# A scheduled attention kernel whose list of steps is given other step times, another order for the steps that empty PSUM, and more zero products

## The chip, the cores and the metric

The kernel runs on one core of one Trainium2 chip. The metric is the device time of one execution in microseconds, as the median of several runs. The engines are TensorE (PE; PEld is its weight load), VectorE (DVE), ScalarE (ACT), GpSimd (POOL) and SyncE (SP, which issues most DMAs).

## The reference

Two attention blocks over the same input are mixed by a gate. Both have 2048 positions, a model width of 512 and 32 heads of 16.

```python
def reference(A_x, A_wqkv, A_wo, B_x, B_wqkv, B_wo, gate_w):
    x = A_x                                              # 1 x 2048 x 512, bf16
    g = _sigmoid((x * gate_w).sum(-1, keepdims=True))
    a = _A_ref(x, A_wqkv, A_wo)    # full attention: softmax(q k^T / 4) v, then @ wo
    b = _B_ref(x, B_wqkv, B_wo)    # each position sees itself and 7 others: back 2, 4, ... 14
    return g * a + (1 - g) * b
```

The full attention has 32 heads x 2048 x 2048 exponentials; they are the bulk of the work.

## The kernel before

**Block A.** Heads are taken in eight groups of four, queries in four chunks of 512. One group with one chunk is a period; the last one is halved. In a period there are 16 key tiles x 4 heads = 64 units. A unit is the scores of 128 keys by 512 queries (one product of TensorE with 32 rows, `qk`), their exponential, and the product with V (`pv`), which adds into an accumulator, one PSUM bank for a period. Four heads stand in four strips of TensorE's rows or columns, so that up to four such products run beside each other.

Most units go to ScalarE in sets of alternately three and two (`set_sizes`): the scores go to a ring in PSUM (`rA` of three banks, `rB` of two), ScalarE writes the exponentials to `pT`. A ring is free again when its exponential is done. Some units go elsewhere instead. VectorE computes the exponential in four passes that read the scores' bank (`p1` to `p4`, tiles `dg` and `pd`): each needs the one before. GpSimd does the same with a cubic after a copy by VectorE (`g1`, then `g2` to `g4`, tiles `gt`). A unit taken so is a block; its scores are a `dq` product.

**PSUM.** Five banks are the two rings. The other three (`bank`, tag `m`) serve everything else: the accumulator, the blocks' scores, and the results of all projections, which VectorE copies out.

**Block B.** For each of 16 tiles of 128 positions K, V and Q are projected and copied (`kvs`, `qb`); K and V go to DRAM and come back shifted (`sh`); GpSimd does products and sums, with a small softmax between (`mx`, `lg`, `rr`). The gate's products go through DRAM as well (`zd`, `zfin`) and meet the outputs at their normalisation.

**The list.** The order on each engine is not the program's own: every step is an `Op` with an engine, an assumed time `occ`, a due time `dl`, the steps that it needs (`deps`), and the buffers that it takes and uses. `Scheduler.run` plays the program through with these times. At each turn it looks which engine can start a step first, and takes, among the steps of that engine that can start within `AHEAD`, the one with the lowest `key` (its due time, shifted by the drift of the whole list). `Feeder` adds the sets and the blocks while the list is being made: a new block is asked for when few passes of the last are left, so a VectorE that the list thinks faster gets more blocks, and ScalarE fewer sets. `t1` spreads the periods' due times. The result is an order for each engine. The chip keeps that order and its own times: TensorE, for example, stands at a product whose bank isn't free, with all that is listed behind it. `pick_pe` tries to keep the scores ahead of other products when the exponential would come late; a product whose strips are free costs only `JOIN` there, 0.05, and another kind of product `SWITCH` more.

A pass that needs another step on its own engine could start, in the list before, at that step's end:

```python
o.ready = max([o.rel] + [d.end if d.eng == o.eng and o.eng in ("dve", "act", "pool") else d.done for d in o.deps]
              + [d.t for d in o.after])
```

**Zero products.** After the list is made, `add_zeros` looks at each stretch of `SPAN` = 3.42 us. Where TensorE's work takes less than the share `STREAM` of it, it puts products of zeros (`z`), which add nothing to an open accumulator, into gaps of TensorE's list.

**Steps that come up later.** `sel` (tile `selp`, from `kmp`) runs four times, once for each two groups of heads, as a maximum of four numbers and a scaled mask on VectorE. `k_pack` and `q_pack` project the K and Q of two groups at a time into `kpk` and `qpk`.

Nearly every instruction is recorded at one line, that of the helper which keeps the order (L379 in the profile of before), so groups are told apart by tiles.

Of the kernel before, what the change touches and what calls it, by code (L numbers as in the profile page):

```python
# [21 lines left out]
    t1=848.0,  # L22
# [13 lines left out]
NG = 8  # L36
# [69 lines left out]
SPAN, STREAM, SPARE, ROOM, FREE = 3.42, 0.49, 0.32, 0.1, 0.3  # L106
WARM = 13
WAVE, SWITCH, JOIN = 0.222, 0.10, 0.05
# [10 lines left out]
SET_LAT = 0.52  # L119
EARLY = 4  # L120
ACC = 100
SLOW = 1.5


class Scheduler:
# [56 lines left out]
    def key(self, o):  # L182
        return o.dl - (ACC if o.role == "acc" else 0.0) if o.role else o.dl + self.drift
# [145 lines left out]
def kernel(  # L329
# [85 lines left out]
    UNIT = 0.459  # L415
# [100 lines left out]
    o_init_d = op("dve", 2.2, init_dve, -9.0, deps=[o_init_z])  # L516
# [71 lines left out]
    o_kr, o_qr = {}, {}  # L588
# [6 lines left out]
    for sc in range(NC):  # L595
# [28 lines left out]
        km0_ops.append(op("dve", 0.7, km, -5.0 + sc, deps=[a, o_init_d], use=[tk]))  # L624
# [19 lines left out]
    def q_direct(c_, dl):  # L644
# [32 lines left out]
        a = op("dve", 1.1, qc, dl + 0.9, deps=[a] + o_cr[:1], use=[tk_q] + ([] if fold else [qt_tok[0]]),  # L677
# [7 lines left out]
        o_qr[0, c_] = [op("dve", 0.7, qe, dl + 3.0, deps=[a], alloc=[qt_tok[0]] if fold else [],  # L685
# [20 lines left out]
        st_f["rx"], st_f["th"] = op("dve", 1.4, rx, dl + 5.0, deps=[a, o_fpv], alloc=[t_h], use=[t_f, acc_tok["f"]]), t_h  # L706
# [7 lines left out]
    def k_pack(cc):  # L714
# [3 lines left out]
        for sc in range(NC):  # L718
# [23 lines left out]
            evs.append(op("dve", 0.7, kc, dl + 1.5, deps=[a], alloc=[] if sc else [tp], use=[tk] + ([tp] if sc else []),  # L742
                          after=pk_last[:]))
            pk_last[:] = evs[-1:]
            kms.append(op("dve", 0.7, km, dl + 3.0, deps=[evs[-1]], use=[tp]))
# [5 lines left out]
        kv_p[cc] = op("dve", 0.35, sel, dl + 4, deps=kms + [o_init_p3], slack=SLOW)  # L751
# [14 lines left out]
    def q_pack(cc):  # L766
# [5 lines left out]
        for c in range(NC):  # L772
# [18 lines left out]
            evs.append(op("dve", 0.7, qc, dl + 1.5, deps=[a], alloc=[] if c else [tp], use=[tk] + ([tp] if c else []),  # L791
# [19 lines left out]
        b = op("dve", 0.7, be, dl + 3.5, deps=[prev], alloc=[tbn], use=[tb])  # L811
# [33 lines left out]
    def v_proj(h0, h1, tb, TB, dl, rel, w, dep, use=(), P=2):  # L845
# [21 lines left out]
        c = op("dve", 0.75, ev, dl + 1.7, deps=[a, o_init_p if h1 <= 8 else o_init_p3], use=[tk])  # L867
# [31 lines left out]
    a = op("dve", 0.7, ze, 37.0, deps=[a], alloc=[tzo], use=[tkz])  # L899
# [34 lines left out]
    def b_tile(t):  # L934
# [29 lines left out]
        ka = op("dve", 0.71, ke, tb - 13, deps=[a], use=[tk, tkv])  # L964
# [3 lines left out]
        va = op("dve", 0.71, ve, tb - 11, deps=[a, ka], use=[tk, tkv])  # L968
# [9 lines left out]
        qa = op("dve", 0.71, qe, tb - 5, deps=[a], use=[tk, tqb])  # L978
# [83 lines left out]
        a = op("dve", 0.45, sm_pre, tb + 21, deps=[l1], alloc=[tmx], use=[tlg])  # L1062
        a = op("pool", 0.65, sm_sub, tb + 22, deps=[a], use=[tlg, tmx], lat=1.5)
        a = op("act", 0.3, sm_exp, tb + 24, deps=[a], use=[tlg])
        a = op("dve", 0.78, sm_post, tb + 25, deps=[a], alloc=[trr], use=[tlg])
# [15 lines left out]
        o_obt.append(op("dve", 0.44, oe, tb + 65, deps=[a], use=[tk]))  # L1081
# [80 lines left out]
    class Feeder:  # L1162
# [45 lines left out]
        def new_set(self, s):  # L1208
# [45 lines left out]
            b = Op("act", 0.427 * n + 0.081, ex, now + 1.0, deps=[a], alloc=[tp], use=[tr_], name=f"ex{k}", role="ex")  # L1254
# [98 lines left out]
        def d_passes(self, s, e):  # L1353
# [50 lines left out]
            if e == "d":  # L1404
                ps_ = [Op("dve", 0.69, p1, x + 1.0, deps=[o], alloc=[tg], use=[tk], role="d", name="p1")]
                ps_.append(Op("dve", 0.69, p2, x + 1.1, deps=ps_[-1:], use=[tk, tg], role="d", name="p2"))
                ps_.append(Op("dve", 0.69, p3, x + 1.2, deps=ps_[-1:], use=[tk, tg], role="d", name="p3"))
                ps_.append(Op("dve", 0.69, p4, x + 1.3, deps=ps_[-1:], alloc=[tp], use=[tk, tg], role="d", name="p4", slack=0.4))
            else:
                ps_ = [Op("dve", 0.69, g1, x - 2.0, deps=[o], alloc=[tg, tp], use=[tk], role="d", name="g1")]  # L1410
# [19 lines left out]
    for pi, (c_, i, q0, qn) in enumerate(periods):  # L1430
# [39 lines left out]
        a = op("dve", 0.75 * f if pi else 1.45, po1, E - 1.0, deps=[o_end[pi]] + ([] if pi else [st_f["rx"]]), alloc=[ta],  # L1470
               use=[acc_tok[pi]] + ([] if pi else [st_f["th"]]))
        a = op("dve", 0.4 if last else 0.25, po2, E + 2.0, deps=[a, o_g], alloc=[trd], use=[ta])
        a = op("dve" if last else "pool", 0.27 if last else 0.95, po2b, E + 3.0 if last else E + 2.5, deps=[a],
               alloc=[to] if par == 0 else [], use=[ta, trd] + ([to] if par else []))
        if par:
            o_oat[pr, c_, q0] = op("dve", 0.75 * f, po3, E + 4.0 if i == NG - 1 else E + 12.0, deps=[a], use=[to])

    st_fa = {}
    for t in range(NT):
# [40 lines left out]
        if fa:  # L1520
# [15 lines left out]
            fa0 = op("dve", 0.71, to_fa, dl, deps=[a] + ([fa0] if tt else []), alloc=[] if tt else [tfa], use=[tk] + ([tfa] if tt else []))  # L1536
# [3 lines left out]
            a = op("dve", 0.71, t_ev, dl, deps=[a, fa0], alloc=[tos], use=[tk2, tfa])  # L1540
# [5 lines left out]
        a = op("act" if on_act else "dve", 0.65 if on_act else 0.71, f_ev, dl + (1.0 if late else 0.0), deps=[a], alloc=[tos], use=[tk])  # L1546
# [40 lines left out]
```

## Time and profile before

| | us |
|---|---|
| median of three runs | 863.15 |
| the three runs | 866.37, 862.37, 863.15 |
| the profiled execution | 867.63 |
| its span, first to last instruction | 865.9 |
| mean granted TensorE clock | 0.988 |

In the rows of the profile, a group shows its tiles as written<-read, the shapes, the count, the busy time and the mean duration in ns, and the idle time before it with what ended it. A row of a timeline has the start, the length and what ran, with a count where several are merged. A row of a window has the stretch, its length, the busy time of each engine with the number of its instructions, the granted clock, the share of DMA and GB/s. A row of waits has who waited for whom: the sum in us, how often, the longest.

### The profile page before, as it was taken

The numbers are of one execution on the slowest core, as the hardware profiler recorded it, in microseconds if no ns is written. First come the engines' busy times: TensorE is split into PE (matmuls) and PEld (weight loads), VectorE is DVE, ScalarE is ACT, GpSimd is POOL, SyncE is SP. The second block draws the span as 40 slices with busy tenths as digits, with TensorE's granted clock in tenths as the row PEclk, the third lists the DMA queues.
The fourth block names the chain that finished last, engine by engine and source line by source line (L and its number), as shares of the span: only waits on it lengthen the run. The fifth ranks groups of instructions, "written<-read, shape, count | busy, mean of one in ns | idle before, by whom it ended". The sixth has DMA issues, their size and how long they took to land.

```text
span 865.9 us, 18130 instructions
## 1 busy us (share of the span) xinstructions
PE 794.5 (92%) x7145; PEld 258.5 (30%) x7145; DVE 749.8 (87%) x1235; ACT 841.4 (97%) x750; POOL 714.0 (82%) x588
## 2 busy tenths in 40 slices
PE   8999999998889998999999998989889889999997
PEld 3323333322223332222223332222222223222233
DVE  6788889889999998798999889898999986888875
ACT  5999999999999999899999999999999999999996
POOL 2086998899799989996998999899989768888772
PEclk9999999999999998899999999999999999999999
DMA  9432203231321113123113111323110000000000
GB/s 224 134 90 89 81 7 77 95 79 39 106 72 64 49 62 74 38 49 111 50 37 111 50 62 19 117 68 93 50 50 25 1 2 13 13 14 14 8 14 32
DMA packets 54781, 51.56 MB, mean 60 GB/s; under 512 B 13628, under 2 KB 51172, under 8 KB 54696
## 3 DMA queue, kind: packets, MB, share of 16 engines
q1 hardware_dynamic: 53496, 50.11, 20.1%
q8 instruction: 56, 0.92, 0.4%
q10 hardware_dynamic: 1200, 0.30, 0.2%
q14 instruction: 29, 0.24, 0.1%
HBM read 38.04 MB, written 6.33 MB: 51 GB/s over the span
## 4 chain that ended last, share of the span: by engine, by line
ACT 58%; issue 19%; PE 17%; DVE 3%; DMA 1%; SPq 1%; ACTq 0%; DVEq 0%
ACT pT L379 58%; PE bank L379 12%; PE ring L379 5%; DVE dg L379 1%; ACT lg L379 1%; DMA xT<-in_A_x_dram 1%; SPq L379 1%; DVE pd L379 0%; DVE kmp L379 0%; DVE kpk L379 0%; DVE rden L379 0%; DVE kvs L379 0%; DVE selp L379 0%; DVE qpk L379 0%; DVE oat L379 0%
## 5 line engine op out<-in xcount | busy, mean ns | idle before, releaser
L379 ACT ACTIVATE pT<-ring 128x1536 bf16<-128x1536 f32 x728 | 835.2, 1279 | 10.5 <-PE ring L379 8.7
L379 PE MATMUL ring<-qt,kt 32*128 32x512 bf16 (+1 forms) x1880 | 291.7, 379 | 42.0 <-ACT pT L379 36.3
L379 PE MATMUL bank<-pT,vp_all 128*17 128x512 bf16 (+2 forms) x1872 | 288.9, 379 | 19.0 <-ACT pT L379 15.5
L379 DVE SCALAR_TENSOR_TENSOR dg<-bank,dg 128x512 bf16<-128x512 uint16 x420 | 289.3, 689 | 12.9
L379 POOL TENSOR_TENSOR prod<-prod 128x1024 f32<-128x1024 f32 x144 | 230.9, 1603 | 11.3
L379 DVE TENSOR_SCALAR dg<-bank 128x512 bf16<-128x512 uint16 x210 | 142.8, 680 | 46.3 <-PE bank L379 33.3
L379 PEld LDWEIGHTS <-kt 32*128 32x128 bf16 x2136 | 96.1, 91 | 278.3 <-issue 272.0
L379 POOL TENSOR_TENSOR prod<-sh,qb 128x1024 f32<-128x1024 bf16 x64 | 135.1, 2132 | 39.0 <-DMA sh<-kv_scr 37.7
L379 PEld LDWEIGHTS <-vp_all 128*17 128x17 bf16 (+1 forms) x2112 | 93.3, 89 | 223.3 <-issue 197.4
L379 DVE TENSOR_TENSOR pd<-bank,dg 128x512 uint16<-128x512 f32 x210 | 144.5, 688 | 6.7
L379 POOL TENSOR_TENSOR prod<-sh,lg 128x1024 f32<-128x1024 bf16 x64 | 127.5, 2014 | 1.8
L379 PE MATMUL bank<-ones_t,z 128*32 128x512 bf16 (+1 forms) x367 | 119.4, 388 | 1.5 <-DVE ones_t L379 1.5
L379 PE MATMUL bank<-qt,kt 32*128 32x512 bf16 (+1 forms) x240 | 87.6, 377 | 2.0 <-DVE kvs L379 0.9
L379 POOL TENSOR_TENSOR gt<-gt 128x512 f32<-128x512 f32 x63 | 75.2, 1194 | 5.2
L379 PE MATMUL bank<-pd,vp_all 128*17 128x512 bf16 (+1 forms) x216 | 75.6, 379 | 0.0
L379 PE MATMUL bank<-bw,xT 128*32 128x512 bf16 x768 | 69.2, 388 | 0.1
L379 POOL TENSOR_SCALAR gt<-gt 128x512 f32<-128x512 uint16 (+2 forms) x63 | 38.9, 617 | 25.8 <-DVE gt L379 18.3
L379 PE MATMUL bank<-xT,wst 128*32 128x512 bf16 x512 | 46.0, 390 | 0.0
L379 PEld LDWEIGHTS <-z 128*32 128x32 bf16 x367 | 29.7, 96 | 37.3 <-issue 30.3
L379 PEld LDWEIGHTS <-xT 128*32 128x32 bf16 (+1 forms) x1088 | 31.6, 96 | 27.0 <-issue 22.3
L379 DVE STREAM_TRANSPOSE accT<-bank 128x512 f32<-128x512 f32 (+1 forms) x32 | 21.9, 686 | 10.3 <-PE bank L379 9.9
L379 DVE CAST kvs<-bank 128x512 bf16<-128x512 f32 x32 | 21.8, 683 | 3.2 <-PE bank L379 2.8
(103 smaller groups left out, 413.4 us busy)
## 6 DMA issues: line engine op xcount, KB each, us to landing
sh<-kv_scr SPq DMA_DIRECT2D x64, 512.0 KB
kv_scr<-kvs SPq DMA_DIRECT2D x16, 256.0 KB
out_dram<-osb SPq DMA_DIRECT2D x15, 128.0 KB
kt<-kpk SPq DMA_DIRECT2D x28, 64.0 KB
qt<-qpk SPq DMA_DIRECT2D x28, 64.0 KB
wst<-in_A_wqkv_dram SPq DMA_DIRECT2D x3, 512.0 KB
bw<-in_B_wqkv_dram SPq DMA_DIRECT2D x1, 1536.0 KB
bwo<-in_B_wo_dram SPq DMA_DIRECT2D x1, 512.0 KB
```

The source lines that it names most:

```text
L379: return chain_on(key, f(*a, **k))
```

## The change

All edits are in the list's numbers and in how it weighs steps; no engine's instructions are written differently. The step times of VectorE and ScalarE are set anew: passes from 0.69 to 0.61, copies from 0.7 to 0.61, an exponential from 0.427 n + 0.081 to 0.426 n + 0.052, `sel` from 0.35 to 1.2. On VectorE a step that needs another one of VectorE can start `RAW` = 0.115 after that one's end. The times from an engine's end to another's start (`LAT`, `SET_LAT`) change a little. A VectorE step without a role (all but the blocks' passes) that uses one of the three banks gets a key lower by `EV` = 100, so that it goes ahead of all else that can start. The blocks' scores are due earlier (`DQ_DL`, `GQ_DL`). `t1` falls from 848 to 828, and `STREAM` rises from 0.49 to 0.54.

```diff
-    t1=848.0,
+    t1=828,
...
+        self.frees = eng == "dve" and not role and any(not tk.res.fifo for tk in use)
...
-LAT = dict(pe=0.25, dve=0.12, act=0.22, pool=2.5, sp=2.2)
-AHEAD = dict(pe=0.10, dve=0.12, act=0.25, pool=0.5, sp=0.0)
+LAT = dict(pe=0.22, dve=0.135, act=0.165, pool=2.5, sp=2.2)
+RAW = 0.115
+AHEAD = dict(pe=0.10, dve=0.1, act=0.25, pool=0.5, sp=0.0)
...
-DQ_DL = 0.4
+DQ_DL = -1
+GQ_DL = -2
...
-SPAN, STREAM, SPARE, ROOM, FREE = 3.42, 0.49, 0.32, 0.1, 0.3
+SPAN, STREAM, SPARE, ROOM, FREE = 3.42, 0.54, 0.32, 0.1, 0.3
...
-SET_LAT = 0.52
+SET_LAT = 0.495
+EV = 100
...
-        o.ready = max([o.rel] + [d.end if d.eng == o.eng and o.eng in ("dve", "act", "pool") else d.done for d in o.deps]
+        o.ready = max([o.rel] + [d.end + (RAW if o.eng == "dve" else 0.0) if d.eng == o.eng and o.eng in ("dve", "act", "pool") else d.done for d in o.deps]
...
-        return o.dl - (ACC if o.role == "acc" else 0.0) if o.role else o.dl + self.drift
+        return o.dl - (ACC if o.role == "acc" else 0.0) if o.role else o.dl + self.drift - (EV if o.frees else 0.0)
...
-            lat = LAT[e] + occ if o.lat is None else o.lat
+            lat = LAT[e] + occ if o.lat is None else o.lat + (max(0.0, occ - o.occ) if e == "pe" else 0.0)
...
-    UNIT = 0.459
+    UNIT = 0.447
...
-        kv_p[cc] = op("dve", 0.35, sel, dl + 4, deps=kms + [o_init_p3], slack=SLOW)
+        kv_p[cc] = op("dve", 1.2, sel, dl + 4, deps=kms + [o_init_p3], slack=SLOW)
...
-            b = Op("act", 0.427 * n + 0.081, ex, now + 1.0, deps=[a], alloc=[tp], use=[tr_], name=f"ex{k}", role="ex")
+            b = Op("act", 0.426 * n + 0.052, ex, now + 1.0, deps=[a], alloc=[tp], use=[tr_], name=f"ex{k}", role="ex")
...
-            o = Op("pe", WAVE, None, max(s.free["pe"], s.free["dve"] - 1.0) + (DQ_DL if e == "d" else 1.5), alloc=[tk],
-                   lat=0.5, kind="r", name=e + "q", role="dq")
+            o = Op("pe", WAVE, None, max(s.free["pe"], s.free["dve"] - 1.0) + (DQ_DL if e == "d" else GQ_DL), alloc=[tk],
+                   lat=0.45, kind="r", name=e + "q", role="dq")
...
-                ps_ = [Op("dve", 0.69, p1, x + 1.0, deps=[o], alloc=[tg], use=[tk], role="d", name="p1")]
+                ps_ = [Op("dve", 0.61, p1, x + 1.0, deps=[o], alloc=[tg], use=[tk], role="d", name="p1")]
...
-                ps_ = [Op("dve", 0.69, g1, x - 2.0, deps=[o], alloc=[tg, tp], use=[tk], role="d", name="g1")]
+                ps_ = [Op("dve", 0.61, g1, x - 2.0, deps=[o], alloc=[tg, tp], use=[tk], role="d", name="g1")]
```

The other edits set further steps of VectorE to their new times in the same way (copies 0.61, `mx` 0.33, `rr` 0.72, `obt` 0.33, the accumulator's transposes 0.64 and 0.63, its reciprocal 0.17).

More of the change, by code (lines that the diff above doesn't have):

```diff
@@ L676, in q_direct @@
             a = op("pe", 0.265 * n, qp(c, n), dl, after=[a], use=[tk_q, tw0])
-        a = op("dve", 1.1, qc, dl + 0.9, deps=[a] + o_cr[:1], use=[tk_q] + ([] if fold else [qt_tok[0]]),
+        a = op("dve", 0.95, qc, dl + 0.9, deps=[a] + o_cr[:1], use=[tk_q] + ([] if fold else [qt_tok[0]]),
                alloc=[ta_q] + tqf)
@@ L684, in q_direct @@
         a = op("pe", 0.25, qb, dl + 2.8, deps=[a, o_selk], alloc=[tk_b], use=[ta_q])
-        o_qr[0, c_] = [op("dve", 0.7, qe, dl + 3.0, deps=[a], alloc=[qt_tok[0]] if fold else [],
+        o_qr[0, c_] = [op("dve", 0.61, qe, dl + 3.0, deps=[a], alloc=[qt_tok[0]] if fold else [],
                              use=[tk_b] + (tqf if fold else [qt_tok[0]]))]
@@ L741, in k_pack @@
             a = op("pe", 2 * WAVE, part(2), dl + 0.5, deps=[a], use=[tk])
-            evs.append(op("dve", 0.7, kc, dl + 1.5, deps=[a], alloc=[] if sc else [tp], use=[tk] + ([tp] if sc else []),
+            evs.append(op("dve", 0.61, kc, dl + 1.5, deps=[a], alloc=[] if sc else [tp], use=[tk] + ([tp] if sc else []),
                           after=pk_last[:]))
             pk_last[:] = evs[-1:]
-            kms.append(op("dve", 0.7, km, dl + 3.0, deps=[evs[-1]], use=[tp]))
+            kms.append(op("dve", 0.61, km, dl + 3.0, deps=[evs[-1]], use=[tp]))
         def sel():
@@ L790, in q_pack @@
             a = op("pe", 2 * WAVE, part(2), dl + 0.5, deps=[a], use=[tk])
-            evs.append(op("dve", 0.7, qc, dl + 1.5, deps=[a], alloc=[] if c else [tp], use=[tk] + ([tp] if c else []),
+            evs.append(op("dve", 0.61, qc, dl + 1.5, deps=[a], alloc=[] if c else [tp], use=[tk] + ([tp] if c else []),
                           after=pk_last[:]))
@@ L810, in be @@
             V.tensor_copy(out=st["n"][:], in_=st["b"][:])
-        b = op("dve", 0.7, be, dl + 3.5, deps=[prev], alloc=[tbn], use=[tb])
+        b = op("dve", 0.61, be, dl + 3.5, deps=[prev], alloc=[tbn], use=[tb])
         def sct(g):
@@ L866, in v_proj @@
             a = op("pe", 0.163 * (h1 - h0) / 4 * TB / P, mk(k), dl + 0.7 / P * k, after=[a], use=[tk] + list(use), busy=0.65)
-        c = op("dve", 0.75, ev, dl + 1.7, deps=[a, o_init_p if h1 <= 8 else o_init_p3], use=[tk])
+        c = op("dve", 0.6, ev, dl + 1.7, deps=[a, o_init_p if h1 <= 8 else o_init_p3], use=[tk])
         for h in range(h0, h1):
@@ L898 @@
     a = op("pe", 0.9, zc, 36.0, deps=[o_bw] + [o for x in o_xt for o in x], alloc=[tkz])
-    a = op("dve", 0.7, ze, 37.0, deps=[a], alloc=[tzo], use=[tkz])
+    a = op("dve", 0.61, ze, 37.0, deps=[a], alloc=[tzo], use=[tkz])
     o_zd = [op("sp", 0.6, zd, 38.0, deps=[a], use=[tzo])]
@@ L963, in b_tile @@
         a = op("pe", 2 * WAVE, proj("pk", 1, 2, tk), tb - 13.5, deps=[a], use=[tk])
-        ka = op("dve", 0.71, ke, tb - 13, deps=[a], use=[tk, tkv])
+        ka = op("dve", 0.61, ke, tb - 13, deps=[a], use=[tk, tkv])
         tk = bank()
@@ L967, in b_tile @@
         a = op("pe", 2 * WAVE, proj("pv", 2, 2, tk), tb - 11.5, deps=[a], use=[tk])
-        va = op("dve", 0.71, ve, tb - 11, deps=[a, ka], use=[tk, tkv])
+        va = op("dve", 0.61, ve, tb - 11, deps=[a, ka], use=[tk, tkv])
         o_kvd.append(op("sp", 0.6, kvd, tb - 10, deps=[va], use=[tkv], lat=3.0))
@@ L977, in b_tile @@
         a = op("pe", 2 * WAVE, proj("pq", 0, 2, tk), tb - 5.5, deps=[a], use=[tk])
-        qa = op("dve", 0.71, qe, tb - 5, deps=[a], use=[tk, tqb])
+        qa = op("dve", 0.61, qe, tb - 5, deps=[a], use=[tk, tqb])
         def load(which, hf):
@@ L1061, in b_tile @@
         tmx, trr = tok("mx", 2), tok("rr", 2)
[L1062 removed]
+        a = op("dve", 0.33, sm_pre, tb + 21, deps=[l1], alloc=[tmx], use=[tlg])
         a = op("pool", 0.65, sm_sub, tb + 22, deps=[a], use=[tlg, tmx], lat=1.5)
         a = op("act", 0.3, sm_exp, tb + 24, deps=[a], use=[tlg])
[L1065 removed]
+        a = op("dve", 0.72, sm_post, tb + 25, deps=[a], alloc=[trr], use=[tlg])
         a0 = op("pool", 8.8, av_half(0), tb + 40, deps=[a, ld[2], o_g], alloc=[tob], use=[tlg, tsh[2], trr], name=f"av{t}")
@@ L1080, in b_tile @@
         a = op("pe", 0.35, fin, tb + 64, deps=[a1], alloc=[tk], use=[tbb], busy=0.6)
-        o_obt.append(op("dve", 0.44, oe, tb + 65, deps=[a], use=[tk]))
+        o_obt.append(op("dve", 0.33, oe, tb + 65, deps=[a], use=[tk]))
     for t in range(NT):
@@ L1469 @@
         f = 0.12 + 0.88 * qn / QW
-        a = op("dve", 0.75 * f if pi else 1.45, po1, E - 1.0, deps=[o_end[pi]] + ([] if pi else [st_f["rx"]]), alloc=[ta],
+        a = op("dve", 0.64 * f if pi else 1.35, po1, E - 1.0, deps=[o_end[pi]] + ([] if pi else [st_f["rx"]]), alloc=[ta],
                use=[acc_tok[pi]] + ([] if pi else [st_f["th"]]))
-        a = op("dve", 0.4 if last else 0.25, po2, E + 2.0, deps=[a, o_g], alloc=[trd], use=[ta])
+        a = op("dve", 0.4 if last else 0.17, po2, E + 2.0, deps=[a, o_g], alloc=[trd], use=[ta])
         a = op("dve" if last else "pool", 0.27 if last else 0.95, po2b, E + 3.0 if last else E + 2.5, deps=[a],
@@ L1475 @@
         if par:
-            o_oat[pr, c_, q0] = op("dve", 0.75 * f, po3, E + 4.0 if i == NG - 1 else E + 12.0, deps=[a], use=[to])
+            o_oat[pr, c_, q0] = op("dve", 0.63 * f, po3, E + 4.0 if i == NG - 1 else E + 12.0, deps=[a], use=[to])
     st_fa = {}
@@ L1535 @@
                 tfa = tok("pk", 2)
-            fa0 = op("dve", 0.71, to_fa, dl, deps=[a] + ([fa0] if tt else []), alloc=[] if tt else [tfa], use=[tk] + ([tfa] if tt else []))
+            fa0 = op("dve", 0.61, to_fa, dl, deps=[a] + ([fa0] if tt else []), alloc=[] if tt else [tfa], use=[tk] + ([tfa] if tt else []))
             tk2 = tail.__defaults__[-1]
@@ L1539 @@
             a = op("pe", 0.26, tail, dl - 1.0, deps=oats(3), alloc=[tk2])
-            a = op("dve", 0.71, t_ev, dl, deps=[a, fa0], alloc=[tos], use=[tk2, tfa])
+            a = op("dve", 0.61, t_ev, dl, deps=[a, fa0], alloc=[tos], use=[tk2, tfa])
             op("sp", 0.6, dout, dl + 1.0, deps=[a], use=[tos], lat=2.2)
@@ L1545 @@
             dl = E + 4.0
-        a = op("act" if on_act else "dve", 0.65 if on_act else 0.71, f_ev, dl + (1.0 if late else 0.0), deps=[a], alloc=[tos], use=[tk])
+        a = op("act" if on_act else "dve", 0.6 if on_act else 0.61, f_ev, dl + (1.0 if late else 0.0), deps=[a], alloc=[tos], use=[tk])
         op("act" if on_act else "sp", 0.6, dout, dl + 2.0, deps=[a], use=[tos], lat=2.2)
```

10 lines of the change are left out of this document (5 added, 5 removed).

## The prediction

> **What bounds the kernel now.** I read the page first (busy times, then the chain that ended last).
>
> ```profile
> span 865.9 us, 18130 instructions
> PE 794.5 (92%) x7145; PEld 258.5 (30%) x7145; DVE 749.8 (87%) x1235; ACT 841.4 (97%) x750; POOL 714.0 (82%) x588
> ...
> ACT 58%; issue 19%; PE 17%; DVE 3%; DMA 1%; SPq 1%; ACTq 0%; DVEq 0%
> ```
>
> ScalarE (ACT) is busy 97% of the span and carries most of the chain; what is left of the chain is products that it waits for. So a step that leaves ACT shortens the kernel, and so does each late product; work on the other engines costs only where it makes ACT late. Next, the groups by form give ACT's work: 363 exponentials of three tiles, 363 of two, 2 of one.
>
> ```profile
> L379 ACT ACTIVATE pT<-ring 128x1536 bf16<-128x1536 f32 x363 | 541.6, 1492 | 7.1 <-PE ring L379 5.9 <-PE bank L379 0.5
> L379 ACT ACTIVATE pT<-ring 128x1024 bf16<-128x1024 f32 x363 | 388.1, 1069 | 3.3 <-PE ring L379 2.8 <-ACT pT L379 0.2
> ...
> L379 ACT ACTIVATE pT<-ring 128x512 bf16<-128x512 f32 x2 | 1.2, 600 | 0.0
> ```
>
> The durations overlap (the tail of one runs under the head of the next), so I need the pace from begin to begin: a clean stretch, as a window of ACT alone and as timeline, then the first exponential and the last ones.
>
> ```profile
> 605.50:623.37 17.87, 17.87 (x17) 1.00 0.18 60
> 605.19 0.45 ACT L379 ACTIVATE lg<-lg 128x256 f32<-128x256 f32 x1
> 605.50 18.22 ACT L379 ACTIVATE pT<-ring 128x1024 bf16<-128x1024 f32 x16
> 10.50 1.45 ACT L379 ACTIVATE pT<-ring 128x1536 bf16<-128x1536 f32 x1 [1.25 <-PE ring L379]
> 856.03 3.14 ACT L379 ACTIVATE pT<-ring 128x1024 bf16<-128x1024 f32 x3
> ```
>
> Sixteen exponentials begin from 605.50 up to 623.37 (the seventeenth begins there): 17.87 / 8 = 2.234 us for a pair of one three-tile and one two-tile step. The mean durations differ by 1.492 - 1.069 = 0.423 us, a tile more, so the three take 1.329, 0.905 and 0.48 us. From 10.50 to 856.03 + 3.14 = 859.17 there are 848.7 us; 363 pairs make 810.9, the two single tiles 1.0, sixteen `lg` steps of 0.31 (605.19 to 605.50) 5.0, three small steps about 2 (an estimate). Some 30 us are ACT waiting for late products, although the page's idle time shows little of it: a step that waits in the pipe shows as a longer one.
>
> I find two sources of these 30 us. The first is one event near 337 us (timeline of all engines, then windows, the first of the exponentials alone).
>
> ```profile
> 335.30 3.78 ACT L379 ACTIVATE pT<-ring 128x1536 bf16<-128x1536 f32 x3 [0.25 <-PE ring L379]
> 335.40 2.33 POOL L379 TENSOR_TENSOR prod<-prod 128x1024 f32<-128x1024 f32 x1
> 335.53 2.23 DVE L379 TENSOR_SCALAR selp<-mask,kmp 128x32 bf16<-128x32 bf16 x1
> 337.68 0.68 DVE L379 CAST kvs<-bank 128x512 bf16<-128x512 f32 x1
> 338.41 0.37 PE L379 MATMUL bank<-qt,kt 32*128 32x512 bf16 x1 [0.89 <-DVE kvs L379]
> 354.98 12.87 ACT L379 ACTIVATE pT<-ring 128x1536 bf16<-128x1536 f32 x11 [0.68 <-PE ring L379]
> 335.25:354.95 19.70, 7.29 (x30) 14.53 (x12) 0.65 0.41 114
> 337.30:340.70 3.40, 2.43 (x33) 0.77 (x30) 2.90 (x6) 2.66 (x3) 3.09 (x5) 1.00 0.72 170
> 340.74:344.15 3.41, 3.26 (x14) 0.65 (x14) 1.94 (x4) 2.92 (x4) 3.41 (x2) 0.50 0.52 181
> ```
>
> VectorE's `selp` begins at 335.53 and ends at 337.76, just after the GpSimd step that ends at 337.73. Behind it the `kvs` copy empties its bank late, the next product stands 0.89 us, TensorE is busy only 2.43 of 3.40 us, and then the granted clock is 0.50. From 335.30 to 354.98 twelve exponentials begin: 19.68 us against 6 x 2.234 = 13.40. The event costs 6.3 us.
>
> The second source is a habit of the list: the product with V (`pv`) that waits for an exponential stands ahead of the scores (`qk`) that wait for the same exponential to free the ring.
>
> ```profile
> 522.12 3.37 ACT L379 ACTIVATE pT<-ring 128x1024 bf16<-128x1024 f32 x3
> 522.30 0.39 PE L379 MATMUL bank<-pT,vp_all 128*17 128x512 bf16 x3
> 522.62 0.39 PE L379 MATMUL ring<-qt,kt 32*128 32x512 bf16 x3
> 523.12 1.45 ACT L379 ACTIVATE pT<-ring 128x1536 bf16<-128x1536 f32 x1
> ```
>
> The scores begin 0.32 behind the `pv`, and the next exponential begins 1.00 after the two-tile one instead of 0.905: 0.1 us lost. In the order of the instructions 118 three-tile sets stand so before: some 12 us. That leaves about 12 us in small waits.
>
> **The change part by part.** What the list becomes I take from the instruction lists of both kernels, what a step costs from rows.
>
> *Work that leaves ACT.* VectorE takes 219 blocks instead of 210, GpSimd 19 instead of 21. ACT keeps 361 three-tile, 363 two-tile and 1 one-tile steps: 2 x 1.329 + 0.48 = 3.1 us less, all of it on the path.
>
> *What VectorE pays.* Its steps from begin to begin, and three waits:
>
> ```profile
> 439.57 0.69 DVE L379 SCALAR_TENSOR_TENSOR dg<-bank,dg 128x512 bf16<-128x512 uint16 x1
> 440.30 0.69 DVE L379 TENSOR_TENSOR pd<-bank,dg 128x512 uint16<-128x512 f32 x1
> 440.90 0.68 DVE L379 TENSOR_SCALAR qb<-bank 128x512 bf16<-128x512 f32 x1
> 442.24 0.69 DVE L379 TENSOR_SCALAR dg<-bank 128x512 bf16<-128x512 uint16 x1 [0.65 <-PE bank L379]
> 442.96 1.42 DVE L379 SCALAR_TENSOR_TENSOR dg<-bank,dg 128x512 bf16<-128x512 uint16 x2
> 444.41 0.69 DVE L379 TENSOR_TENSOR pd<-bank,dg 128x512 uint16<-128x512 f32 x1
> 445.02 0.68 DVE L379 TENSOR_SCALAR dg<-bank 128x512 bf16<-128x512 uint16 x1
> DVE dg L379 <- PE bank L379: 33.3, 54, 1.6
> PE ring L379 <- ACT pT L379: 36.3, 124, 0.6
> PE bank L379 <- ACT pT L379: 15.5, 65, 0.6
> ```
>
> A pass that needs the one before begins 0.725 after it (442.96 to 444.41 is two); one that doesn't, 0.61 (444.41 to 445.02). The new list, which knows this, puts other steps between the passes: 408 passes of the chains stand right behind the one that they need, 566 before. Nine more blocks cost 9 x 4 x 0.61 = 22.0 us, two copies for GpSimd go (1.2), and 158 gaps of 0.115 close (18.2). VectorE needs 2.6 us more; it has 54 waits of 33.3 us in all for its first product, which the new list asks for earlier (DQ_DL from 0.4 to -1). Cost on the path: 0. Without the 18.2 it would still have the 33.3.
>
> The Trainium skill, "VectorE: DVE Perf Modes", section "The DRAIN you can't avoid", says that the next operation starts only when the pipe of the last has emptied, and that waits between them change nothing. By that the 18.2 us would not be won, VectorE would need 20.8 us more against 33.3 of waits, the sum would stay and the slower case would gain chance, 0.25 by my estimate. The rows disagree: 0.725 against 0.61.
>
> *The `selp` step.* The list sets 1.2 us for it instead of 0.35, and behind the third one now stand the last three passes of a block, not the `kvs` copy. It may still be held: its four runs took 234 to 2228 ns.
>
> ```profile
> L379 DVE TENSOR_SCALAR selp<-mask,kmp x4: 234/1060/2228, 48.2 to 545.9; 128x32 bf16<-128x32 bf16 x4
> 335.43 1.04 PE L379 MATMUL bank<-ones_t,z 128*32 128x512 bf16 x4
> PE bank L379 <- DVE osb L379: 0.3, 1, 0.3
> ```
>
> Held for 2.2 it is 1.0 late where it was 1.9 late. Between nothing won and 6.3 us I take 6.3, because no copy that frees a bank stands behind it.
>
> *Zero products.* 400 instead of 367 (the wide ones 394 for 345, the half ones 6 for 22). One takes (1.04 - 0.39) / 3 = 0.22 us, so about 9 us more on TensorE, put where it waits for ACT (36.3 + 15.5 us). If that cover failed it would cost up to 9; but the scores that stand right behind a zero product are 137 sets, 140 before. I take 0.
>
> The Trainium skill, "TensorE: Matmul & The Clock Gate", section "Why this matters for your kernels", asks only that TensorE has no gap over about 3 us. By that the event would cost its stand of 0.89 us and not the clock, and the sum below would be 862.1. The rows disagree: at most 0.97 us of idle time in the window from 337.30, and the clock is 0.50 in the next.
>
> *Steps that free PSUM first.* Of 179 copies that empty a bank, 65 now stand inside a chain of passes, 32 before. What they can win is TensorE's waits for VectorE's copies outside the event, each of 0.3 us or less: I take 0.6. What they can cost is the third rival.
>
> *The `pv` ahead of the scores.* 109 sets instead of 118: 9 x 0.1 = 0.9 us won. This habit stays.
>
> *What else moves.* The gate's small transfers, `zd` and `zfin`, stand a few issues later on SyncE, its loads of shifted K and V one to four places, the `lg` exponentials 7 to 13 steps later on ACT; t1 only shifts due times. GpSimd waits for these, and it is busy 714 of 865.9 us: 0, and without that cover one load's place in the queue.
>
> **The sum.** The profiled execution took 867.63 (span 865.9 and 1.73 around it): 867.63 - 3.1 - 0.9 - 6.3 - 0.6 = 856.7 us. The three runs (862.37 to 866.37, median 863.15) lie below it; without the event it would have taken 861.3, less than any, so I think each run holds a part of the event, and take 856.7 for a run without it: 0.75% under the median.
>
> **The rivals.**
>
> *The event or its like stays.* `selp`, held by a GpSimd step of 2.33 us, costs the clock again somewhere, or the runs of before hold little of it. Then 856.7 + 6.3 = 863.0, no difference. For it: the hold is not taken away, only planned for. Against: no bank waits behind the third `selp`, and TensorE has 33 products more.
>
> *The small waits go too.* A list with true times could also clear the last 12 us: 856.7 - 11 = 846. For it: ACT's and VectorE's true pace in the list. Against: it leaves `pv` ahead of the scores in 109 sets, so its times for TensorE are not the true ones.
>
> *Banks are held longer: slower.* Three banks serve all but the rings, and an accumulator holds one of them. Chains that are interleaved hold two at a time, so a product for a new bank stands on TensorE, and the scores stand behind it in order. If each of the 158 opened places costs 0.11 us of that: 17.4, or 874 us. It decides from 0.07 on (10.8 / 158). For it: at 338.41 exactly such a stand made ACT late. Against: outside the event TensorE waits for VectorE's copies 0.3 us at a time.
>
> **How the numbers follow.** The forecast (855 to 858.5) 0.50; small waits go too (846 to 855) 0.17; event stays (859 to 866) 0.19; slower (868 to 876) 0.14. A measurement of this kernel tells about 0.5% from no change. Faster by more (under 858.8): 0.50 + 0.17 = 0.67; same 0.19; slower (over 867.5) 0.14. The range from 846 to 866 leaves out the slower case and a little of the best.
>
> **What would show it.** Right: 725 exponential steps; the clock at 1.00 from 300 to 400 us; `dg` waits for PE bank well under 33.3; about 110 pairs still 0.1 long. Wrong: PE bank waits for DVE of several us (banks held), a clock of 0.50 behind a `selp`, or pairs over 2.234 without a `pv` between.

## The result, and the profile after

The changed kernel takes 860.4 us (median of ten runs, 858.52 to 862.02) against 863.18 us before (ten runs, 862.12 to 866.85). The ratio is 0.9962, with a 95% interval of 0.9946 to 0.9977: faster by some 0.4%, inside the half per cent that the prediction called no difference and gave a chance of 0.19. The forecast was 856.7, the range 846 to 866. The direction was right and the size less than half.

The page of the profiled execution (859.63 us, span 858.0), with the rows that answer to those of before:

```profile
span 858.0 us, 18198 instructions
PE 795.5 (93%) x7178; PEld 256.6 (30%) x7178; DVE 756.3 (88%) x1269; ACT 837.0 (98%) x747; POOL 704.2 (82%) x576
PEclk9999999999999999999989999999999999999999
...
ACT 58%; PE 22%; issue 17%; DVE 3%; ACTq 0%; DVEq 0%
...
L383 ACT ACTIVATE pT<-ring 128x1536 bf16<-128x1536 f32 x725 | 830.5, 1277 | 7.2 <-PE ring L383 5.1
...
L383 PE MATMUL bank<-ones_t,z 128*32 128x512 bf16 (+1 forms) x400 | 131.8, 390 | 1.5 <-DVE ones_t L383 1.5
```

ScalarE is still the bound: 98% busy, 58% of the chain. It has 725 exponentials instead of 728. TensorE has its 400 zero products. The line of the clock has its one dip in another place than before. A window over the place of the old event in the kernel before:

```profile
300.00:400.00 100.00, 92.99 (x817) 28.39 (x818) 85.07 (x134) 94.35 (x85) 85.42 (x64) 0.93 0.22 58
```

The same window in the changed kernel, one over the new dip, and the four runs of `selp`:

```profile
300.00:400.00 100.00, 94.69 (x831) 29.16 (x825) 92.75 (x153) 99.58 (x90) 91.37 (x66) 1.00 0.31 83
443.27:450.10 6.83, 6.78 (x42) 1.36 (x41) 4.69 (x8) 5.65 (x6) 6.67 (x4) 0.50 0.25 78
L383 DVE TENSOR_SCALAR selp<-mask,kmp x4: 233/432/684, 51.8 to 543.7; 128x32 bf16<-128x32 bf16 x4
```

From 300 to 400 us the clock is now 1.00 and ScalarE is busy 99.58 instead of 94.35 us, and no `selp` is held over 0.68 us. But from 443.27 to 450.10 the clock is 0.50, after two short stands of TensorE (0.49 and 0.67 us). In mid-run the execution of before lost the clock for 13.65 us there and for 3.41 us from 685.49 on; the execution of after loses it once, elsewhere, for 6.83 us. VectorE's chain and its waits:

```profile
334.26 0.69 DVE L383 TENSOR_SCALAR dg<-bank 128x512 bf16<-128x512 uint16 x1 [0.19 <-PE bank L383]
334.87 0.68 DVE L383 TENSOR_TENSOR pd<-bank,dg 128x512 uint16<-128x512 f32 x1
335.46 0.68 DVE L383 SCALAR_TENSOR_TENSOR dg<-bank,dg 128x512 bf16<-128x512 uint16 x1
336.12 0.72 DVE L383 STREAM_TRANSPOSE accT<-bank 128x512 f32<-128x512 f32 x1
DVE dg L383 <- PE bank L383: 18.4, 28, 2.1
PE ring L383 <- ACT pT L383: 28.8, 89, 0.7
PE bank L383 <- ACT pT L383: 14.6, 64, 0.6
```

The first pass of one block (334.26), the last of another (334.87) and the second pass of the first (335.46) follow each other at 0.61 and 0.59 us: this is what the new list does between dependent passes. The first passes wait 18.4 us in 28 places instead of 33.3 in 54. And a late pair, of which there are about as many as before:

```profile
309.27 2.45 ACT L383 ACTIVATE pT<-ring 128x1024 bf16<-128x1024 f32 x2
309.45 0.39 PE L383 MATMUL bank<-pT,vp_all 128*17 128x512 bf16 x3
309.77 0.39 PE L383 MATMUL ring<-qt,kt 32*128 32x512 bf16 x3
310.27 1.45 ACT L383 ACTIVATE pT<-ring 128x1536 bf16<-128x1536 f32 x1
```

The `pv` at 309.45 and the scores 0.32 behind it; the next exponential begins 1.00 after the last instead of 0.905 (the last line is the second exponential of the first line).

The trace of each kernel, as ScalarE's steps from begin to begin against the prediction's clean pace (1.329, 0.905 and 0.48 us for three tiles, two and one): all that ScalarE waited for late products, and of it, outside the first 90 us and the stretches at half clock, the steps over 25 ns late whose scores stand right behind a `pv`:

| | before | after |
|---|---|---|
| late in all, us | 30.1 | 25.7 |
| of it at half clock, with the stands that led to it, us | 7.5 | 2.6 |
| of it behind a `pv`, us (steps) | 10.0 (86) | 11.3 (91) |
| of it in the first 90 us | 4.7 | 5.2 |

### The profile page after: what moved, and what is told of

It reads as the page before. It is cut to its first block, busy times and chain, and to the rows that moved or that the text cites. A ratio compares the mean times of both kernels' runs of the same rounds, so it can differ in the third digit from the quotient of the medians.

```text
span 858.0 us, 18198 instructions
## 1 busy us (share of the span) xinstructions
PE 795.5 (93%) x7178; PEld 256.6 (30%) x7178; DVE 756.3 (88%) x1269; ACT 837.0 (98%) x747; POOL 704.2 (82%) x576
## 4 chain that ended last, share of the span: by engine, by line
ACT 58%; PE 22%; issue 17%; DVE 3%; ACTq 0%; DVEq 0%
ACT pT L383 57%; PE bank L383 16%; PE ring L383 6%; DVE dg L383 1%; ACT lg L383 1%; DVE absq L383 0%; DVE accT L383 0%; DVE qb L383 0%; DVE pd L383 0%; DVE qt L383 0%; ACT kt L383 0%; DVE gt L383 0%; DVE km L383 0%; DVE kpk L383 0%; DVE rr L383 0%
## 5 line engine op out<-in xcount | busy, mean ns | idle before, releaser
L383 PE MATMUL ring<-qt,kt 32*128 32x512 bf16 (+1 forms) x1873 | 295.8, 377 | 33.2 <-ACT pT L383 28.8
L383 DVE SCALAR_TENSOR_TENSOR dg<-bank,dg 128x512 bf16<-128x512 uint16 x438 | 300.1, 685 | 10.1
L383 POOL TENSOR_TENSOR prod<-prod 128x1024 f32<-128x1024 f32 x144 | 231.9, 1611 | 11.3
L383 DVE TENSOR_SCALAR dg<-bank 128x512 bf16<-128x512 uint16 x219 | 148.8, 680 | 24.7 <-PE bank L383 18.4
L383 DVE TENSOR_TENSOR pd<-bank,dg 128x512 uint16<-128x512 f32 x219 | 149.6, 683 | 4.1
L383 PE MATMUL bank<-ones_t,z 128*32 128x512 bf16 (+1 forms) x400 | 131.8, 390 | 1.5 <-DVE ones_t L383 1.5
L383 PE MATMUL bank<-qt,kt 32*128 32x512 bf16 (+1 forms) x247 | 91.2, 375 | 1.9 <-DVE qb L383 0.6
L383 POOL TENSOR_TENSOR gt<-gt 128x512 f32<-128x512 f32 x57 | 68.1, 1194 | 4.4
L383 POOL TENSOR_SCALAR gt<-gt 128x512 f32<-128x512 uint16 (+2 forms) x57 | 35.3, 620 | 24.5 <-DVE gt L383 20.3
L383 POOL TENSOR_TENSOR rr<-rr,omg 128x32 f32<-128x32 f32 x16 | 3.9, 242 | 34.7 <-DVE rr L383 25.5
```

What stands on the lines that cost most here:

```text
L383: return chain_on(key, f(*a, **k))
```

## The experiments

Theory W: the time is ScalarE's work plus its late pairs plus what the clock takes; a change of the list is worth what it does to these three. Its rivals are named with each run. Each run is compared with runs of the kernel before on the same chip; where it is set against the changed kernel, the chips may differ (the kernel before has medians from 862.9 to 864.2 beside these runs). Each run also tells its mean granted clock, and from it the time at half clock, 2 x (1 - clock) x time. A step of ScalarE is called late when it begins over 25 ns behind the clean pace.

| | ScalarE's steps (3, 2, 1 tiles) | sets with `pv` ahead | late behind `pv` in the trace | zero products | median us | ratio to before, 95% interval |
|---|---|---|---|---|---|---|
| before | 363, 363, 2 | 118 | 86 | 367 | 863.2 | |
| after | 361, 363, 1 | 109 | 91 | 400 | 860.4 | 0.9962, 0.9946 to 0.9977 |
| E1 | 363, 363, 2 | 118 | 92 | 522 | 863.8 | 1.0006, 0.9991 to 1.0021 |
| E2 | 361, 363, 1 | 109 | 87 | 276 | 866.5 | 1.0024, 0.9996 to 1.0052 |
| E3 | 362, 363, 1 | 123 | 91 | 423 | 866.5 | 1.0032, 1.0018 to 1.0047 |
| E4 | 362, 363, 2 | 32 | 24 | 251 | 854.0 | 0.9888, 0.9865 to 0.9912 |
| E5 | 361, 361, 2 | 119 | 102 | 342 | 857.0 | 0.9922, 0.9906 to 0.9938 |
| E6 | 365, 365, 2 | 121 | 99 | 319 | 869.6 | 1.0063, 1.0040 to 1.0086 |
| E7 | 364, 365, 1 | 24 | 19 | 230 | 856.9 | 0.9927, 0.9905 to 0.9950 |
| E8 | 362, 363, 1 | 18 | 9 | 321 | 852.5 | 0.9870, 0.9849 to 0.9892 |
| E9 | 360, 362, 1 | 112 | 94 | 346 | 856.8 | 0.9925, 0.9900 to 0.9950 |
| E10 | 359, 359, 1 | 8 | 14 | 354 | 863.1 | 0.9991, 0.9975 to 1.0007 |
| E11 | 357, 357, 1 | 14 | 25 | 402 | 880.1 | 1.0184, 1.0158 to 1.0210 |
| E12 | 354, 354, 1 | 19 | 38 | 449 | 899.0 | 1.0411, 1.0381 to 1.0441 |

**E1: the zero products alone.**

```diff
-SPAN, STREAM, SPARE, ROOM, FREE = 3.42, 0.49, 0.32, 0.1, 0.3
+SPAN, STREAM, SPARE, ROOM, FREE = 3.42, 0.54, 0.32, 0.1, 0.3
```

> The kernel before with STREAM at 0.54 and nothing else: the list is the same but for 522 zero products instead of 367. Theory W (the change's 2.8 us are the 3.1 us of exponentials that left ScalarE; the late pairs with pv ahead of the scores stay, and the clock event only moved): the 118 late sets stay, the clock stays at 1.00 in mid-run, and since the runs of before hold only a part of the event the time is 861 to 863 us. Rival Z (the gain comes from the zero products, that is from the clock): 860 us or less, as the changed kernel. Rival C (zero products get in the way of the scores): over 864.

863.81 us against 862.93: above theory W's 861 to 863 and rival Z's 860, just under rival C's 864. The clock did get better: the runs have a mean of 0.994 to 0.999, the 29 runs of before 0.985 to 0.998. But five runs of before at 0.998 take 861.27 to 861.71, and the two of E1 at 0.998 take 863.27 and 863.58: at the same clock 155 zero products more cost some 1.9 us, 0.012 us each. (Lines through all runs, time against time at half clock, give 860.4 and 862.3 at full clock, the same 1.9.) They won the clock and paid as much for it. Rival Z is out for this kernel; rival C is right in kind.

E1 has the list of before, so its trace also tests the `selp` event:

```profile
336.70 2.06 DVE L379 TENSOR_SCALAR selp<-mask,kmp 128x32 bf16<-128x32 bf16 x1
338.68 0.68 DVE L379 CAST kvs<-bank 128x512 bf16<-128x512 f32 x1
339.40 0.37 PE L379 MATMUL bank<-qt,kt 32*128 32x512 bf16 x1 [0.88 <-DVE kvs L379]
337.47:340.88 3.41, 2.54 (x16) 0.57 (x14) 2.95 (x4) 2.70 (x4) 3.17 (x4) 1.00 0.66 142
340.88:344.30 3.42, 3.27 (x38) 1.26 (x37) 2.77 (x7) 3.42 (x4) 3.34 (x3) 1.00 0.67 230
```

`selp` is held for 2.06 us, the `kvs` copy stands behind it, and TensorE stands 0.88 us (0.89 before) and is busy for 2.54 of 3.41 us (2.43 of 3.40 before). Yet the clock stays at 1.00. From 330 to 360 us ScalarE is late by 1.8 us in E1 and by 6.9 in the execution of before. So of the event's 6.3 us the held `selp` costs one to two, and the fall of the clock the rest, and a held `selp` need not make the clock fall.

**E2: the changed kernel with fewer zero products.**

```diff
-SPAN, STREAM, SPARE, ROOM, FREE = 3.42, 0.54, 0.32, 0.1, 0.3
+SPAN, STREAM, SPARE, ROOM, FREE = 3.42, 0.49, 0.32, 0.1, 0.3
```

> The changed kernel with STREAM back at 0.49: the same list with 276 zero products instead of 400. Theory W: the gain stays but for a clock event or two of 1 to 3 us each, 860 to 863 us. Rival Z: the gain is gone, 863 us or more. Rival C: faster than the changed kernel, under 860.

866.53 us, and the widest spread of all: 858.12 at a clock of 0.995 to 870.75 at 0.966. That misses theory W's 860 to 863; in the median rival Z (863 or more) has it. In the profiled execution there are six stretches at half clock before the end; the two longest, as windows:

```profile
636.39:650.04 13.65, 13.65 (x79) 2.62 (x77) 10.49 (x17) 12.06 (x11) 13.18 (x9) 0.50 0.13 41
749.03:766.09 17.06, 17.06 (x77) 2.81 (x75) 12.02 (x20) 13.41 (x12) 12.83 (x16) 0.50 0.00 0
```

Twelve exponentials fall into the second, 17.06 us, where 6 x 2.234 = 13.4 would do. A line through the twelve runs gives 856.5 us at full clock and 0.24 us for each us at half clock; the changed kernel's three runs at the clock of E2's fastest, 0.995, take 859.63 to 860.10 where E2 takes 858.12. So rivals Z and C each had a part of it: for this list the zero products are needed (276 are too few), and each costs some 0.015 us, a figure that rests on one run of E2.

**E3: no step goes ahead for PSUM.**

```diff
-EV = 100
+EV = 0
```

> The changed kernel with EV at 0: steps that free PSUM no longer go first. ScalarE then has one three-tile step more (362, 363, 1), 1.3 us, and 123 three-tile sets have pv ahead instead of 109, 1.4 us. Theory W: 860.4 + 2.7, that is 862 to 864 us. Rival B (freeing banks late costs TensorE waits): 866 us or more, with waits of TensorE for VectorE's copies in the trace. Rival N (freeing first costs time): under 860.

866.55 us, more than theory W allows. The trace shows why, and it isn't a bank (timeline of ScalarE, TensorE and SyncE):

```profile
70.83 0.41 ACT L383 ACTIVATE lg<-lg 128x256 f32<-128x256 f32 x1
76.97 1.02 ACT L383 ACTIVATE pT<-ring 128x1024 bf16<-128x1024 f32 x1 [5.73 <-PE ring L383]
71.94 0.39 PE L383 MATMUL bank<-qt,kt 32*128 32x512 bf16 x1 [2.02 <-DMA qt<-bnd]
69.04 3.29 SPq L383 DMA_DIRECT2D qt<-bnd  x6
```

TensorE stands 2.02 us at a block's scores whose Q rows are still in a transfer, the clock falls to 0.50 at 72.98, and ScalarE has nothing for 5.73 us. Without these 5.73 us the run would be near 861, by my estimate. Such a stand is what this list happened to make, so E3 does not tell what freeing first is worth; E9 asks that again.

**E4: a true price for a product that joins another.**

```diff
-        if o.strips is not None and not (set(o.strips) & self.pe_strips):
+        if o.strips is not None and not (set(o.strips) & self.pe_strips) and (t is None or t < self.free["pe"] + 0.1):
             return JOIN
...
-                    self.pe_strips = set()
-                if o.strips is not None:
-                    self.pe_strips |= set(o.strips)
+                    self.pe_strips = set()
+                self.pe_strips |= set(range(4) if o.strips is None else o.strips)
```

(The condition before these lines also empties the strips where TensorE stood for 0.1 us.)

> The changed kernel with one thing in the list's times for TensorE mended: a product that joins another in free strips costs 0.05 only if the other had free strips and TensorE hasn't stood in between; else 0.222. The list then puts pv ahead of the scores in 32 three-tile sets instead of 109; ScalarE keeps 362, 363 and 2 steps (1.8 us more), and there are 251 zero products instead of 400. Theory W: 77 x 0.1 = 7.7 us fewer late pairs, + 1.8, + up to 3 for the clock: 854 to 858 us, and the late pairs in the trace fall to some 30 behind a pv. Rival P (TensorE is full, the pairs are late whatever stands first): 860 to 863, with as many late pairs behind something else.

853.98 us, at the lower end of what theory W said (854 to 858) and far from its rival. The list had put `pv` ahead because it priced it at 0.05 us there. Now the scores go first:

```profile
159.78 1.07 ACT L382 ACTIVATE pT<-ring 128x1024 bf16<-128x1024 f32 x1
160.13 0.39 PE L382 MATMUL ring<-qt,kt 32*128 32x512 bf16 x3
160.45 0.84 PE L382 MATMUL bank<-pT,vp_all 128*17 128x512 bf16 x5
160.69 1.51 ACT L382 ACTIVATE pT<-ring 128x1536 bf16<-128x1536 f32 x1
```

The next exponential begins 0.91 after the two-tile one. In the trace 24 late steps stand behind a `pv` instead of 91, and ScalarE's lateness in all falls from 25.7 to 18.4 us, though it has 1.8 us more work.

**E5: VectorE's times alone.** Of the change VectorE's step times, `RAW` and VectorE's `LAT` and `AHEAD` are left, and the new `lat` of TensorE's products (0.45 for the blocks' scores).

```diff
-EV = 100
+EV = 0
-DQ_DL = -1
-GQ_DL = -2
+DQ_DL = 0.4
+GQ_DL = 1.5
...
-            b = Op("act", 0.426 * n + 0.052, ex, now + 1.0,
+            b = Op("act", 0.427 * n + 0.081, ex, now + 1.0,
```

(`LAT` of pe and act, SET_LAT, UNIT, t1 and STREAM are set back to before's as well.)

> The changed kernel with all but VectorE's part set back: VectorE's step times and the 0.115 for dependent passes stay, ScalarE's times, the due times of the blocks' scores, t1, EV and STREAM are those of before. The list gives 222 blocks to VectorE and 19 to GpSimd, ScalarE keeps 361, 361 and 2 steps, 4.5 us less than before; 119 sets with pv ahead, 342 zero products. Theory W (the time follows ScalarE's work and the late pairs): 863 - 4.5 and some 1 to 2 for a lost clock, 858 to 861 us. Rival D (blocks beyond before's are paid for by TensorE's waits for VectorE): 863 us or more.

857.02 us: this part alone is faster than the whole change, and 1 us below theory W's 858 to 861. Rival D is out. ScalarE has 4.5 us less work, its lateness is 24.4 us in all, and the clock is 0.995 to 0.998.

**E6: ScalarE's times alone.**

```diff
-LAT = dict(pe=0.25, dve=0.12, act=0.22, pool=2.5, sp=2.2)
+LAT = dict(pe=0.25, dve=0.12, act=0.165, pool=2.5, sp=2.2)
...
-            b = Op("act", 0.427 * n + 0.081, ex, now + 1.0,
+            b = Op("act", 0.426 * n + 0.052, ex, now + 1.0,
```

(UNIT and t1 as in the change.)

> The kernel before with ScalarE's true times in the list alone (0.426 n + 0.052, its latency 0.165, UNIT 0.447, t1 828): the list hurries ScalarE, gives VectorE 205 blocks and GpSimd 16, and ScalarE keeps 365, 365 and 2 steps, 4.5 us more than before; 121 sets with pv ahead, 319 zero products. Theory W: 866 to 869 us. Rival A (true times for ScalarE bring it nearer to its pace by themselves): 862 us or less, with fewer late pairs in the trace.

869.60 us, some 6 us slower and just above theory W's 866 to 869; rival A is out. The true pace of ScalarE in the list does nothing for ScalarE's pace on the chip: 99 late steps stand behind a `pv`. What the edit does, `t1` and `UNIT` included, is to make ScalarE look quick, so that the list gives it 4.5 us more to do.

**E7: the true price in the list before.** The edit of E4 (all its lines), in the kernel before.

```diff
-        if o.strips is not None and not (set(o.strips) & self.pe_strips):
+        if o.strips is not None and not (set(o.strips) & self.pe_strips) and (t is None or t < self.free["pe"] + 0.1):
             return JOIN
```

> The kernel before with the mended price of a joined product alone. pv stands ahead of the scores in 24 three-tile sets instead of 118; ScalarE has 364, 365 and 1 steps, 2.7 us more; 230 zero products instead of 367. Theory W: 94 x 0.1 = 9.4 us fewer late pairs, + 2.7, some us for the clock: 856 to 860. Rival S (the slack that the old list gives ScalarE is what is lost, not the order of two products): 862 or more.

856.87 us, as theory W said (856 to 860), with 19 late steps behind a `pv` instead of 86. The habit is not the change's; mending it is worth as much in either list.

**E8: E4 with accumulators in turn and some more zero products.**

```diff
-ACC = 100
+ACC = 1.5
-SPAN, STREAM, SPARE, ROOM, FREE = 3.42, 0.54, 0.32, 0.1, 0.3
+SPAN, STREAM, SPARE, ROOM, FREE = 3.42, 0.58, 0.32, 0.1, 0.3
```

> The changed kernel with the mended price of a joined product, the first products of an accumulator no longer ahead of everything (ACC 1.5 instead of 100) and STREAM at 0.58. 18 sets with pv ahead (32 without the second edit), ScalarE has 362, 363 and 1 steps, 321 zero products. Theory W: 854.0 - 1.4 - 0.5, and the clock nearer to 1 for some zero products more: 851 to 853 us. Rival A (an accumulator that starts late holds up the sets behind it): 855 or more.

852.45 us, as theory W said (851 to 853), and all four runs have a clock of 0.999 or 1.000: the best version here, 1.3% under the kernel before (interval 1.1 to 1.5%). It makes two edits at once, so it does not tell what each is worth. Nine late steps are left behind a `pv`, and ScalarE's lateness in all is 14.9 us.

**E9: freeing first, on E5.**

```diff
-EV = 0
+EV = 100
```

> The kernel of VectorE's times alone (e5) with EV at 100 added. ScalarE has 360, 362 and 1 steps, 0.9 us less; 112 sets with pv ahead instead of 119, 0.7 us; 346 zero products, 342 there. Theory W: 857.0 - 1.6, 855 to 856 us. Rival B (a bank that is freed late holds TensorE, so freeing first is worth more than its list): 853 or less. Rival N (freeing first delays the chains): 858 or more.

856.78 us, ratio 0.9925 against E5's 0.9922. That is above theory W's 855 to 856 and cannot be told from no change; both rivals are out. Putting the steps that free PSUM first is worth nothing that these runs show.

**E10 to E12: fewer and fewer steps on ScalarE.** E5's list with the edits of E4 and E8 (`STREAM` at 0.56), `EV` and the due times of the blocks' scores of the change, and ScalarE set slower in the list, here as in E10 (0.44 n + 0.12 in E11, 0.45 n + 0.14 in E12; t1 and UNIT with it):

```diff
-            b = Op("act", 0.427 * n + 0.081, ex, now + 1.0,
+            b = Op("act", 0.433 * n + 0.1, ex, now + 1.0,
```

> VectorE's times, EV at 100, the early due times of the blocks' scores, the mended price of a joined product, ACC 1.5, STREAM 0.56, and ScalarE set slower than it is in the list (0.433 n + 0.1, t1 860, UNIT 0.465), so that it gets fewer sets: 359, 359 and 1 steps; 229 blocks on VectorE and 23 on GpSimd; 8 sets with pv ahead; 354 zero products. Theory W: from e8's 852.5, 7.6 us less work, 1 us for late pairs, 0.4 for zero products: 843 to 846 us. VectorE needs some 805 us by its steps, so it isn't the bound. Rival D (VectorE at 95% already makes TensorE wait): 849 or more.

> As e10 with ScalarE slower still in the list (0.44 n + 0.12, t1 875, UNIT 0.475): 357, 357 and 1 steps, 236 blocks on VectorE and 26 on GpSimd, 14 sets with pv ahead, 402 zero products. Theory W: 841 us by ScalarE's work; VectorE needs some 823 us, 98% of that. Rival D: VectorE's waits come back on ScalarE, 845 or more.

> As e10 with ScalarE slower yet in the list (0.45 n + 0.14, t1 890, UNIT 0.485): 354, 354 and 1 steps, 248 blocks on VectorE and 29 on GpSimd, 19 sets with pv ahead, 449 zero products. By ScalarE's work alone it would take 835 us. VectorE needs some 855 us (772 of the changed kernel, 29 blocks of 2.44, 49 gaps of 0.115, 10 copies). Theory W with VectorE as the next bound (rival D here): 858 to 870 us, slower than e10. Rival E (VectorE's steps overlap more than their begins tell): under 850.

863.13, 880.12 and 898.95 us: theory W failed in E10 and E11, and E12 lies even beyond the 858 to 870 that I gave for VectorE as the bound. Rival D's times held in E10 and E11, and so earlier than I had worked out; in E12 its sign is right and its size too small. What TensorE waited for in E10 and E12, and ScalarE's waits for GpSimd there:

```profile
PE ring L382 <- ACT pT L382: 30.2, 88, 1.4
PE bank L382 <- DVE accT L382: 2.6, 7, 0.5
PE bank L382 <- DVE pd L382: 2.5, 8, 0.5
ACT lg L382 <- POOL lg L382: 5.8, 5, 1.6
```

```profile
PE bank L382 <- DVE pd L382: 30.0, 68, 1.0
PE ring L382 <- ACT pT L382: 11.5, 22, 1.8
PE bank L382 <- DVE accT L382: 5.8, 14, 0.9
ACT lg L382 <- POOL lg L382: 9.6, 9, 2.0
```

Summed over its rows, TensorE waits for VectorE 5.9 us in E8 (217 blocks), 6.1 in E5 (222), 19.2 in E10 (229), 42.0 in E11 (236) and 64.6 in E12 (248). In E12 there are 68 waits for the last pass of a block (`pd`): the block's product with V stands on TensorE, and the scores stand behind it. ScalarE's work falls by 16 us from E5 to E12 and its lateness rises from 24.4 to 79.7.

VectorE is not the only cause. From E8 to E10 the time rises by 10.6 us with 7.6 less work, so ScalarE is late by some 18 us more. TensorE's waits for VectorE grow by 13.3 us; ScalarE itself stands 5.8 us at `lg` steps that GpSimd, with 23 blocks instead of 18, has not made ready (no such wait in E8); and the clock is 0.981 to 0.990 instead of 0.999 to 1.000. These overlap, and no run here separates them.

## Why the prediction was right or wrong

*Work that leaves ScalarE: right.* 725 steps, 3.1 us. E5 and E6 show that the time follows this term, down and up by 4.5 us of work each, with 1 to 2 us besides, as long as no other engine makes ScalarE wait (E10). One aside was wrong: a step that waits for its input does not show as a longer one. The late three-tile step at 523.12 took 1.45 us, under the mean of 1.492. What hides the waits is that durations overlap by 0.16 us (1.492 - 1.329), so a step less late than that leaves no idle time.

*What VectorE pays: right.* It takes nine blocks more and waits 18.4 us for its first products instead of 33.3. The Trainium skill's "VectorE: DVE Perf Modes", section "The DRAIN you can't avoid", says that an operation starts only when the pipe of the last has emptied, but also that one which is not held starts earlier. The prediction left the second out. Here passes follow each other at 0.61 and 0.59 us when none needs the one right before it, and at 0.725 when it does.

*The `selp` event: the term that failed.* I took all 6.3 us of the profiled execution as won. The stretch from 300 to 400 us is clean, as I said, but in part by luck: I reckoned with a `selp` that is still held, and in this execution the third one, at 329.24, took 0.57 us. And E1 shows that the hold was not what cost most: with the same hold and the same stand the clock stayed at 1.00. The size was wrong twice. First, the median run of before did not hold the event in full: its 29 runs lie at clocks of 0.985 to 0.998, a line through them gives 860.4 us at full clock, and their median is 862.9, so the clock costs 2.5 us there. I had written that each run holds a part of the event and still took it off whole from the profiled execution. Second, the clock falls elsewhere instead: the ten runs of after lie at 0.987 to 0.997, a line through them gives 858.4 at full clock, and their median is 860.4, so 2.0 us are still lost. The term was 2.5 - 2.0 = 0.5 us, not 6.3. It is uncertain by about as much: the runs of before beside E5 to E8 and E9 to E12 give 861.2 at full clock with medians of 863.3 and 864.2, so 2.1 and 3.0 us. Of the rival "the event or its like stays" the second half is what happened, at 860.4 instead of 863.0.

*Zero products: a cost left out.* I put them at nothing. By E1 and E2 each costs 0.012 to 0.015 us, so 33 more cost 0.4 to 0.5 by this estimate, and they are no surplus: E2 without 124 of them is slower by 5 to 6 us in the median. The cover that I named, TensorE's waits for ScalarE, holds for most of a product's 0.22 us, not for all.

*`pv` ahead of the scores: right in kind, wrong in sign.* I foresaw that the habit stays. It did, but instead of 0.9 us less it costs 11.3 us instead of 10.0, since there are 91 late steps instead of 86 in fewer listed sets. In E4, E7 and E8, where the mended price puts `pv` ahead in 32, 24 and 18 sets, 24, 19 and 9 late steps are left: they come from the order.

*Freeing first: 0.6 us taken, nothing shown* (E9).

*The sum.* 3.1 for the work, 0.5 for the clock, against it 1.3 for late pairs and 0.4 for zero products: 1.9 us of the 2.8 measured. The remaining 0.9 is not settled; the interval of the ratio is 2.7 us wide, and the late pairs may hold part of what the zero products cost. Between the two profiled executions the sum closes better: 3.1 for the work and 30.1 - 25.7 = 4.4 for lateness make 7.5 of the 7.9 us between their spans. The prediction was built on the execution of before, which at 867.63 us is slower than each of its ten runs.

*The rivals.* That the small waits go too was out: the late steps stayed. That banks are held longer is not seen in the changed kernel, but E10 shows how near it was: with 229 blocks instead of E8's 217, TensorE's waits for VectorE treble.

## What to carry to other kernels

A list's step times decide two things, which step goes first and which engine gets the work. For the times of VectorE and ScalarE the second was worth more here, and the true time of the busiest engine made things worse by handing it more (E6, with its due times). Where a wait ends with an order of two products, mend the price that chose that order: that one edit was worth 6 us, more than all of the change. A loss that one profiled execution shows is worth only what the median run loses by it, so hold it against the spread of the runs and their clocks first. And a cause read from one trace (the held `selp`) wants a second run in which the same thing happens.

## What the runs showed of the hardware

The granted clock varies from run to run of one kernel with nothing changed (0.985 to 0.998 in 29 runs of before), and it accounts for most of their spread of 5.5 us: 0.24 to 0.26 us for each us at half clock where the spread is wide (before, E2), 0.16 in the changed kernel. The Trainium skill's "TensorE: Matmul & The Clock Gate", section "Why this matters for your kernels", asks for no idle gap of TensorE over about 3 us if the clock is to stay up. In E3 it fell after one of 2.02 us, and in the first profile after no more than 0.97 us of idle time in 3.40. With 0.87 us of 3.41 idle at the same place E1 kept its clock; what decides between these two, no run here shows.

I had not expected VectorE to make others wait so early. Its steps, summed at the prices of the prediction, need some 805 of E10's 860.5 us (an estimate; the profile's page has it busy for 781.8), and yet with 12 blocks more than in E8 what TensorE waits for it has trebled.
